# Backward of sliding-window attention on one core: its operations as one list per engine, ordered by positions

## The chip, the cores and the metric

The program runs on one core of a Trainium2 chip. The metric is the device time of one execution in microseconds, from the first to the last instruction and what lies around them. The core has five instruction queues that run side by side and wait for one another through semaphores: TensorE (PE, matmuls; PEld in the profile is its weight loads), VectorE (DVE), ScalarE (ACT), GpSimd (POOL) and SyncE (SP, which only issues DMAs here). Each queue runs its instructions in the order in which the program has them.

## The reference, cut to what matters

Four layers run forward and then backward: linear attention (A), sliding-window attention (B), A, B. The change touches only the backward of the scores of layer kind B, which runs twice.

```python
def _B_ref(x, wqkv, wo):
    B, S, D = x.shape                  # 1, 2048, 640
    H = 32; Dh = D // H; W = 256       # 32 heads of 20
    qkv = (lambda x, *d: x.transpose(*d))((x @ wqkv).reshape(B, S, 3, H, Dh), 2, 0, 3, 1, 4)
    q, k, v = qkv[0], qkv[1], qkv[2]
    scores = jnp.einsum("bhqd,bhkd->bhqk", q, k) * (Dh ** -0.5)
    idx = jnp.arange(S)
    mask = (idx[:, None] - idx[None, :] >= 0) & (idx[:, None] - idx[None, :] < W)
    scores = jnp.where(mask[None, None], scores, -1e9)
    p = _softmax(scores, axis=-1)
    o = jnp.einsum("bhqk,bhkd->bhqd", p, v)
    ...
x = x + _A_ref(_layernorm(x, axis=-1), A_wqkv, A_wo)
x = x + _B_ref(_layernorm(x, axis=-1), B_wqkv, B_wo)
x = x + _A_ref(_layernorm(x, axis=-1), A_wqkv, A_wo)
x = x + _B_ref(_layernorm(x, axis=-1), B_wqkv, B_wo)
...
_out, _vjp = jax.vjp(_f, A_x, A_wqkv, A_wo, B_wqkv, B_wo)
_grads = _vjp(grad_out)
```

For each head the backward needs the weights e = exp(scores) again, the product dP = dO V^T (its inputs are prepared beforehand so that dS = dP * e), and from them dQ = dS K, dK = dS^T Q and dV = e^T dO.

## The kernel before, in words

`B_attn_bwd` does this part. It is called twice, for layer 3 (761 us to 1088 us in the profiled execution) and for layer 1 (1501 us to 1822 us); what lies before, between and after the two calls is the same code in both kernels.

**Tiling.** The sequence is cut into 16 tiles of 128 rows (`TT`), the 32 heads into 8 groups of 4 (`G`). A head has 20 columns, padded to 32 (`HPAD`), so that the four heads of a group lie in four strips of 32 rows of the PE array. A query tile t meets the key tiles t-2, t-1 and t: three blocks of 128x128 to a head. A group has 15 steps (`NB`; the first step takes query tiles 0 and 1 together), a call has 120 steps (`NS`). A step n works on two pairs of heads, p = 0 and p = 1, numbered h = 2n + p. "Position" below is n modulo 15.

**The operations of a pair**, with the lines of the kernel before:

- S: scores, two matmuls from `QT` and `KT`, each in a strip of 32 rows (L1563). They go to `pair0`, `pair1` or `pair2` in PSUM, two banks each.
- X: exp on ACT, from that bank to `e_sb` (L1583). M: two masks on POOL (L1587, L1590).
- DP: two matmuls from `dOT` and `VT` (L1563) into the same PSUM bank, after X has read it.
- DS: `ds_sb` = bank * `e_sb` on DVE (L1598). It frees the bank for S of the pair three further on.
- T: dS turned. Either six transposes on PE into `dsT_ps`, a single PSUM bank (L1611), and then C, a copy to `dsT` on ACT (pair 0) or on DVE (pair 1) (L1615); or one DMA transpose from `ds_sb` to `dsT`, issued by SP (in the helper at L326). Pair 0 is always turned on PE. Pair 1 is turned by DMA at 11 of 15 positions (all but 0, 2, 4 and 6), and by PE in the last six steps of a call.

**The operations of a unit** (one group and one tile t, three steps after the step that has query tile t):

- A: the narrow products. For each head up to nine matmuls of 128x128 against 32 columns (L1627 for dQ, L1631 for dK and dV) into `dqvk_ps`, one PSUM bank. They need `dsT` of the step three back (for pair 1 in heads 2 and 3).
- EV: DVE scales the bank into `dqkv` (L1636) and frees it. 128 EV belong to a call.

Two units, the last of a group and the first of the next, fall into position 2.

**The order** is written out in one loop over h under `tc.manual_schedule`; the engines' queues take the operations in the order of the code. In one turn of the loop: DS(h), S(h+3), DP(h+2), X(h+3) with M(h+3), T(h), then the DVE copy of the pair before, EV of the unit that is done, the ACT copy if h is even, and half of the unit's heads. So PE has S and DP of two different pairs next to each other, then six transposes (if any), then 18 narrow matmuls; that twice a step. The `ds_sb` ring has 5 buffers, `e_sb` 7, `dsT` 8, `dsT_ps` and `dqvk_ps` one each.

**SP** also issues the seven slab loads of the next group, four of them DMA transposes (`QTg`, `KTg`, `VTg`, `dOTg`) and three plain (`Ksl`, `Qsl`, `dOsl`), at positions 0, 2, 4, ..., 12, each ahead of the step's own dS; and weights (`wq`) at positions 9 and 14 (layer 3) or in the last group (layer 1). In the last group the next phase's first loads stand between them in SP's queue.

## Time and profile before

| what | us |
|---|---|
| three timed runs | 2197.92, 2197.25, 2187.54 (median 2197.25) |
| the profiled execution | 2190.22 |
| its span, first to last instruction | 2188.3 |
| first to last EV, layer 3 | 776.2 to 1088.5 |
| first to last EV, layer 1 | 1514.8 to 1821.3 |
| DS on DVE, one | 0.949 |
| X on ACT, one | 0.812 |
| C on ACT, one; on DVE | 0.797; 0.558 |
| a mask on POOL, one | 0.406 |
| EV on DVE, one | 0.408 |
| DMA transpose of dS: issue on SP, median | 1.24 |

Every line of a timeline below has the start, the duration, engine, line, operation, output and input with their shapes, the number of instructions merged into it, and in brackets how long the engine stood idle before it and who ended that. The start of one EV to the start of the next is the length of a step.

### The profile page before, as it was taken

How to read it: one execution, taken by the hardware profiler on the slowest of the kernel's cores; microseconds unless marked ns; L12 is line 12 of the kernel's file. 1: busy time of each engine (PE TensorE's matmuls, PEld its weight loads, DVE VectorE, ACT ScalarE, POOL GpSimd, SP SyncE). 2: the span in 40 equal slices, each digit the busy share in tenths (PEclk: the TensorE clock that was granted, in tenths of full speed). 3: DMA queues.
4: the chain of work that ended last, by engine and by line, in shares of the span. 5: the costliest groups of instructions: out<-in, count | busy, mean ns of one | idle time of the engine just before them, and what ended most of it. 6: DMA issues, size and time to landing. Idle time of an engine off the chain costs nothing. (4 is left out here: it accounts for less than half of the span.)

```text
span 2188.3 us, 67939 instructions
## 1 busy us (share of the span) xinstructions
PE 1996.8 (91%) x27856; PEld 1392.4 (64%) x27856; DVE 1435.9 (66%) x2950; ACT 1200.1 (55%) x1981; POOL 879.3 (40%) x1850
## 2 busy tenths in 40 slices
PE   6878899879999789999899999998999999998999
PEld 4655666556666566676656667646676666666774
DVE  6766667577776288888734458705888885444651
ACT  4627777627778388888622223314989882120430
POOL 1015556516777355555423213202656551231220
PEclk9989999999999899999999999999999999999999
DMA  7459989569998499989888799936989996999954
GB/s 261 166 140 198 196 190 191 120 188 199 213 201 193 100 154 158 161 162 162 170 192 182 188 193 213 194 94 131 160 149 162 148 183 147 195 191 220 187 114 102
DMA packets 947802, 375.70 MB, mean 172 GB/s; under 512 B 828321, under 2 KB 928289, under 8 KB 947105
## 3 DMA queue, kind: packets, MB, share of 16 engines
q1 hardware_dynamic: 869712, 297.55, 71.3%
q10 hardware_dynamic: 77776, 73.79, 11.2%
q8 instruction: 218, 3.57, 0.7%
q14 instruction: 96, 0.78, 0.1%
HBM read 106.56 MB, written 112.07 MB: 100 GB/s over the span
## 5 line engine op out<-in xcount | busy, mean ns | idle before, releaser
L1598 DVE TENSOR_TENSOR ds_sb<-pair,e_sb 128x768 bf16<-128x768 f32 x480 | 436.6, 949 | 26.6 <-PE pair L1563 22.9
L1583 ACT ACTIVATE e_sb<-pair 128x768 bf16<-128x768 f32 x480 | 386.4, 812 | 85.2 <-PE pair L1563 81.6
L807 POOL TENSOR_SCALAR_AFFINE_SELECT e_sb<-e_sb 128x384 bf16<-128x384 bf16 (+1 forms) x512 | 198.4, 406 | 369.5 <-ACT e_sb L798 341.2
L798 ACT ACTIVATE e_sb<-s_ps 128x1152 bf16<-128x1152 f32 (+2 forms) x256 | 273.8, 1069 | 108.9 <-PE s_ps L794 79.1
L1590 POOL TENSOR_SCALAR_AFFINE_SELECT e_sb<-e_sb 128x256 bf16<-128x256 bf16 x448 | 182.1, 406 | 246.6 <-ACT e_sb L1583 239.5
L1054 PE MATMUL dw_ps<-dqkv,om 128*128 128x480 bf16 x1280 | 268.8, 366 | 0.0
L1054 PEld LDWEIGHTS <-om 128*128 128x128 bf16 x1760 | 170.1, 98 | 152.0 <-DMA om<-o 9.0
L1242 POOL TENSOR_TENSOR gw<-w,gcar 128x640 f32<-128x640 f32 x64 | 89.4, 1398 | 427.6 <-ACT w L1239 413.7
L1587 POOL TENSOR_SCALAR_AFFINE_SELECT e_sb<-e_sb 128x256 bf16<-128x256 bf16 x512 | 206.5, 407 | 95.5 <-ACT e_sb L1583 95.2
L1054 PEld LDWEIGHTS <-dqT 128*128 128x128 bf16 x1920 | 186.8, 98 | 73.9 <-DMA dqT<-dqkv 0.6
L1615 ACT COPY dsT<-dsT_ps 128x768 bf16<-128x768 bf16 x240 | 191.2, 797 | 24.0 <-PE dsT_ps L1611 7.2
L1611 PE MATMUL dsT_ps<-ident,ds_sb 128*128 128x128 bf16 x1896 | 165.2, 225 | 17.0 <-ACT dsT L1615 15.4
L439 PE MATMUL mm_ps<-Wqkv_B,hnTB 128*128 128x320 bf16 x960 | 171.0, 310 | 8.1 <-DVE gcar L511 5.5
L1627 PEld LDWEIGHTS <-dsT 128*128 128x128 bf16 x2880 | 154.4, 97 | 37.5 <-issue 31.2
L1627 PE MATMUL dqvk_ps<-Ksl,dsT 128*128 128x32 bf16 x2160 | 168.3, 178 | 7.9 <-DMA dsT<-ds_sb 4.9
L1631 PE MATMUL dqvk_ps<-Qsl,ds_sb 128*128 128x32 bf16 x2160 | 165.4, 177 | 0.0
L1631 PE MATMUL dqvk_ps<-dOsl,e_sb 128*128 128x32 bf16 x2160 | 165.3, 177 | 0.0
L1611 PEld LDWEIGHTS <-ds_sb 128*128 128x128 bf16 x1896 | 116.7, 100 | 72.1 <-issue 70.3
L1631 PEld LDWEIGHTS <-ds_sb 128*128 128x128 bf16 x2880 | 145.2, 96 | 0.0
L1631 PEld LDWEIGHTS <-e_sb 128*128 128x128 bf16 x2880 | 144.8, 96 | 0.0
L812 POOL TENSOR_SCALAR_AFFINE_SELECT e_sb<-e_sb 128x512 bf16<-128x512 bf16 x224 | 142.6, 637 | 0.0
L801 ACT ACTIVATE e_sb<-s_ps 128x384 bf16<-128x384 f32 (+2 forms) x256 | 119.9, 469 | 39.1 <-PE s_ps L794 10.5
(209 smaller groups left out, 3949.5 us busy)
## 6 DMA issues: line engine op xcount, KB each, us to landing
qkvp<-qk_slab SPq DMA_DIRECT2D x64, 256.0 KB, 3.5
hn<-hn SPq DMA_DIRECT2D x64, 160.0 KB, 3.2
om<-hn SPq DMA_DIRECT2D x20, 512.0 KB, 5.3
qkvp<-v_slab SPq DMA_DIRECT2D x32, 256.0 KB, 3.7
o<-o SPq DMA_DIRECT2D x48, 160.0 KB, 3.2
om<-o SPq DMA_DIRECT2D x15, 512.0 KB, 5.1
Ksl<-qkvp SPq DMA_DIRECT2D x12, 512.0 KB, 5.3
Qsl<-qkvp SPq DMA_DIRECT2D x12, 512.0 KB, 5.1
```

The costliest lines, as they stand in the source:

```text
L439: nc.tensor.matmul(ps.t[:, w0:w0 + width], lhsT=lhsT(), rhs=rhs(), start=start, stop=stop)
L798: op("ACT", av(3 * nkt * P), lambda: nc.scalar.activation(e.t[:, 0:3, 0:nkt, :], s3.t[:, :, 0:nkt * P].rearrange("p h (i q) -> p h i q", q=P),
L807: nc.gpsimd.affine_select(out=v, in_=v, compare_op=ALU.is_ge, fill=0.0, base=0, pattern=[[0, h1 - h0], [1, P]], channel_multiplier=-1)
L1054: nc.tensor.matmul(ps.t[:, w0:w0 + width], lhsT=lhsT(), rhs=rhs(), start=start, stop=stop)
L1583: nc.scalar.activation(e, PR[h][:, :, 0:3 * P].rearrange("p i (j q) -> p i j q", q=P), ACT.Exp, scale=self.c_att)
L1587: nc.gpsimd.affine_select(out=e[:, :, j, :], in_=e[:, :, j, :], compare_op=ALU.is_ge, fill=0.0, base=0, pattern=[[0, 2], [-1, P]], channel ...
L1590: nc.gpsimd.affine_select(out=e[:, :, j, :], in_=e[:, :, j, :], compare_op=ALU.is_ge, fill=0.0, base=-1, pattern=[[0, 2], [1, P]], channel ...
L1598: nc.vector.tensor_mul(DS[n][:, hs], PR.pop(h)[:, :, 0:3 * P].rearrange("p i (j q) -> p i j q", q=P), E[n][:, hs])
L1611: nc.tensor.transpose(ps[:, i, j, :], DS[n][:, 2 * p + i, j, :], self.ident)
L1615: (nc.vector.tensor_copy if h % 2 else nc.scalar.copy)(TSB[h], TPS.pop(h))
L1627: nc.tensor.matmul(a[:, 0, hh, :], lhsT=TSB[2 * n + hh // 2][:, hh % 2, j, :], rhs=ld[g]["K"][:, k, cs], start=(i == 0), stop=(i == len(dq ...
L1631: nc.tensor.matmul(a[:, 1 + x, hh, :], lhsT=src[n][:, hh, j, :], rhs=ld[g][rhs][:, q, cs], start=(i == 0), stop=(i == len(dkv) - 1))
```

## The change

The loop that wrote the order out is gone. Each operation is put into the list of its engine with a position in steps, n plus a constant from the table `ATTN`; each list is sorted by position. The lists are then emitted so that an operation comes after those that it depends on. The positions fix, for each step n in the middle of a group, these cyclic orders:

- PE: DP0(n+1), A heads 1 and 0 of unit n, S0(n+2), DP1(n+1), T1(n) if it is on PE, A heads 3 and 2 of unit n, S1(n+2), T0(n+1).
- DVE: DS0(n+1), C1(n) if any, EV(n), DS1(n+1).
- ACT: C0(n), X0(n+2), X1(n+2). POOL: M0(n+2), M1(n+2).
- SP: the DMA transpose of pair 1 at DS1's position; a slab load for the next group just after that of its own step.

At position 2, which has two units, each unit's four heads stand together: T0(2), the first unit, DP0(3), S0(4), DP1(3), the second unit, S1(4), T0(3).

The table `TURN` says by position how the two pairs are turned: A is PE with a copy on ACT, D is PE with a copy on DVE, F is the DMA. Pair 1 is F at all positions but 5, 6 and 10, and D in the last three steps of a call. That makes 93 DMA transposes of dS in a call where there were 82, and 147 groups of six PE transposes where there were 158; the DVE copies go from 38 to 27. All other operations, their shapes and their numbers are as before, and so are the rings of buffers.

```diff
+    ATTN = dict(S=[-1.794, -1.317],
+                X=[-1.605, -1.429],
+                DP=[-1.045, -0.72],
+                DS=[-0.982, -0.288],
+                T=[-0.152, 0.293],
+                CA=[0.37, 0.207],
+                CD=[-0.808, 0.062],
+                A=[0.152, -0.038, 0.437, 0.345],
+                A2=[-0.11, 0.608],
+                EV=0.26,
+                EV2=[-0.158, 0.258])
+    TURN = ["AF", "AF", "AF", "AF", "AF", "AD", "AD", "AF", "AF", "AF", "AD", "AF", "AF", "AF", "AF"]
...
-                if p == 1 and n % NB not in (0, 2, 4, 6) and n < NS - 6:
+                if by == "F":
                     self.dma_t(t.rearrange("p i j q -> p (i j) q"),
                                DS[n][:, 2 * p:2 * p + 2].rearrange("p i j q -> p (i j q)"))
                     return
...
+            for n in range(NS):
+                for p in range(2):
+                    h = 2 * n + p
+                    by[h] = TURN[n % NB][p] if n < NS - 3 else "AD"[p]
+                    op("PE", n + AT["S"][p], ("S", h), lambda h=h: score(h), [("DS", h - 3)] if h >= 3 else [])
+                    op("ACT", n + AT["X"][p], ("X", h), lambda h=h: weights(h), [("S", h)] + (users(n - 7) if not p else []))
+                    op("POOL", n + AT["X"][p], ("M", h), lambda h=h: masks(h), [("X", h)])
+                    op("PE", n + AT["DP"][p], ("DP", h), lambda h=h: by_head(h, PR[h], "dOT", "VT"), [("X", h)])
+                    op("DVE", n + AT["DS"][p], ("DS", h), lambda h=h: product(h),
+                       [("DP", h), ("M", h)] + (users(n - 5) if not p else []))
+                    free = [("DS", h)] + users((h - 8) // 2)
+                    if by[h] == "F":
+                        op("SP", n + AT["DS"][p], ("T", h), lambda h=h: turned(h, "F"), free)
+                    else:
+                        op("PE", n + AT["T"][p], ("T", h), lambda h=h: turned(h, "P"), free)
+                        op("ACT" if by[h] == "A" else "DVE", n + AT["CA" if by[h] == "A" else "CD"][p], ("C", h),
+                           lambda h=h: copied(h, by[h]), [("T", h)])
...
+                        at = AT["A2"][i] if len(us) == 2 else AT["A"][hh]
+                        op("PE", n + at, ("A", g, t, hh), lambda g=g, t=t, hh=hh: narrow(g, t, hh), deps)
+                    op("DVE", n + (AT["EV2"][i] if len(us) == 2 else AT["EV"]), ("EV", g, t),
+                       lambda g=g, t=t: evac(g, t), [("A", g, t, hh) for hh in range(4)])
...
+                    op("SP", (g - 1) * NB + 2 * i - 0.001, ("L", g, i), lambda g=g, i=i: slab(g, i), gone if g > 1 else [])
...
+            queue = {e: [name for _, _, name in sorted(v, key=lambda it: it[:2])] for e, v in lists.items()}
...
-                for h in range(2 * (NS + 4)):
-                    n, p = divmod(h, 2)
...
-                    if here:
-                        dve_ds(h)
-                        mm_s(h + 3)
-                        mm_dp(h + 2)
-                        act_exp(h + 3)
-                        turn(h)
...
-                    if (h - 1) % 2:
-                        copy_t(h - 1)
-                    for o in done:
-                        evac(*o)
...
-                    if not p:
-                        copy_t(h)
...
-                        mm_acc(*o, heads)
...
+                while any(queue.values()):
+                    before = len(done)
+                    for names in queue.values():
+                        while names and all(d in done for d in made[names[0]][1]):
+                            done.add(names[0])
+                            made[names.pop(0)][0]()
+                    assert len(done) > before
```

More of the change, by code (lines that the diff above doesn't have):

```diff
@@ L1565, in by_head, with op, score, weights @@
                                          start=True, stop=True, tile_position=(HPAD * hh, 0))
-            def mm_s(h):
-                if h < 2 * NS:
-                    PR[h] = pps.tile([P, 2, 512], F32, name=f"pair{h % 3}")
-                    by_head(h, PR[h], "QT", "KT")
-            def mm_dp(h):
-                if h < 2 * NS:
-                    by_head(h, PR[h], "dOT", "VT")
-            def act_exp(h):
-                if h >= 2 * NS:
-                    return
+            lists = {e: [] for e in ("PE", "DVE", "ACT", "POOL", "SP")}
+            made, bank = {}, {}
+            def op(eng, at, name, f, deps=()):
+                lists[eng].append((at, len(lists[eng]), name))
+                made[name] = (f, list(deps))
+            def score(h):
+                PR[h] = pps.tile([P, 2, 512], F32, name=f"pair{h % 3}")
+                by_head(h, PR[h], "QT", "KT")
+            def weights(h):
                 n, p = divmod(h, 2)
-                if n not in E:
+                if not p:
                     E[n] = pe.tile([P, 4, 3, P], BF, name="e_sb", bufs=7)
+                nc.scalar.activation(E[n][:, 2 * p:2 * p + 2],
+                                     PR[h][:, :, 0:3 * P].rearrange("p i (j q) -> p i j q", q=P), ACT.Exp,
+                                     scale=self.c_att)
+            def masks(h):
+                n, p = divmod(h, 2)
                 e = E[n][:, 2 * p:2 * p + 2]
-                nc.scalar.activation(e, PR[h][:, :, 0:3 * P].rearrange("p i (j q) -> p i j q", q=P), ACT.Exp,
-                                     scale=self.c_att)
                 for j, (t, k) in enumerate(blocks(n)):
@@ L1591, in act_exp, with product @@
                                                 base=-1, pattern=[[0, 2], [1, P]], channel_multiplier=-1)
-            def dve_ds(h):
+            def product(h):
                 n, p = divmod(h, 2)
-                if n not in DS:
+                if not p:
                     DS[n] = pe.tile([P, 4, 3, P], BF, name="ds_sb", bufs=5)
@@ L1599, in dve_ds, with turned @@
                                      E[n][:, hs])
-            def turn(h):
+            def turned(h, by):
                 n, p = divmod(h, 2)
                 t = TSB[h] = pe.tile([P, 2, 3, P], BF, name="dsT", bufs=8)
-                if p == 1 and n % NB not in (0, 2, 4, 6) and n < NS - 6:
+                if by == "F":
                     self.dma_t(t.rearrange("p i j q -> p (i j) q"),
@@ L1611, in turn, with copied, narrow @@
                         nc.tensor.transpose(ps[:, i, j, :], DS[n][:, 2 * p + i, j, :], self.ident)
-            def copy_t(h):
-                if h in TPS:
-                    (nc.vector.tensor_copy if h % 2 else nc.scalar.copy)(TSB[h], TPS.pop(h))
-            def mm_acc(g, t, hhs):
+            def copied(h, by):
+                (nc.scalar.copy if by == "A" else nc.vector.tensor_copy)(TSB[h], TPS.pop(h))
+            def narrow(g, t, hh):
                 if (g, t) not in ACC:
@@ L1621, in mm_acc, with sources @@
                 a = ACC[g, t]
-                dq = [(k, *place(g, t, k)) for k in range(max(t - 2, 0), t + 1)]
-                dkv = [(q, *place(g, q, t)) for q in range(t, min(t + 3, TT))]
-                for hh in hhs:
-                    cs = slice(HPAD * hh, HPAD * (hh + 1))
-                    for i, (k, n, j) in enumerate(dq):
-                        nc.tensor.matmul(a[:, 0, hh, :], lhsT=TSB[2 * n + hh // 2][:, hh % 2, j, :],
-                                         rhs=ld[g]["K"][:, k, cs], start=(i == 0), stop=(i == len(dq) - 1))
-                    for x, (src, rhs) in enumerate(((DS, "Q"), (E, "dO"))):
-                        for i, (q, n, j) in enumerate(dkv):
-                            nc.tensor.matmul(a[:, 1 + x, hh, :], lhsT=src[n][:, hh, j, :],
-                                             rhs=ld[g][rhs][:, q, cs], start=(i == 0), stop=(i == len(dkv) - 1))
+                dq, dkv = sources(g, t)
+                cs = slice(HPAD * hh, HPAD * (hh + 1))
+                for i, (k, n, j) in enumerate(dq):
+                    nc.tensor.matmul(a[:, 0, hh, :], lhsT=TSB[2 * n + hh // 2][:, hh % 2, j, :],
+                                     rhs=ld[g]["K"][:, k, cs], start=(i == 0), stop=(i == len(dq) - 1))
+                for x, (src, rhs) in enumerate(((DS, "Q"), (E, "dO"))):
+                    for i, (q, n, j) in enumerate(dkv):
+                        nc.tensor.matmul(a[:, 1 + x, hh, :], lhsT=src[n][:, hh, j, :],
+                                         rhs=ld[g][rhs][:, q, cs], start=(i == 0), stop=(i == len(dkv) - 1))
+            def sources(g, t):
+                return ([(k, *place(g, t, k)) for k in range(max(t - 2, 0), t + 1)],
+                        [(q, *place(g, q, t)) for q in range(t, min(t + 3, TT))])
             def evac(g, t):
@@ L1639, in evac, with users @@
                     ACC.pop((g, t))[:, :, :, 0:DH], self.ckv.rearrange("p s (h d) -> p s h d", d=DH))
+            def users(n):
+                return [("A", n // NB, n % NB + 1, hh) for hh in range(4)] if n >= 0 else []
+            AT, TURN = self.ATTN, self.TURN
+            by = {}
+            for n in range(NS):
[15 more added lines that the diff above has]
+                           lambda h=h: copied(h, by[h]), [("T", h)])
             outs = {}
@@ L1644, in B_attn_bwd @@
                     outs.setdefault(g * NB + t + 2, []).append((g, t))
+            for n, us in outs.items():
+                for i, (g, t) in enumerate(us):
+                    dq, dkv = sources(g, t)
+                    for hh in range(4):
+                        pair = hh // 2
+                        deps = [("DS", 2 * m + pair) for _, m, _ in dkv]
+                        deps += [("T" if by[2 * m + pair] == "F" else "C", 2 * m + pair) for _, m, _ in dq]
+                        at = AT["A2"][i] if len(us) == 2 else AT["A"][hh]
+                        op("PE", n + at, ("A", g, t, hh), lambda g=g, t=t, hh=hh: narrow(g, t, hh), deps)
+                    op("DVE", n + (AT["EV2"][i] if len(us) == 2 else AT["EV"]), ("EV", g, t),
+                       lambda g=g, t=t: evac(g, t), [("A", g, t, hh) for hh in range(4)])
             if first is None:
@@ L1649, in B_attn_bwd, with slab @@
                 ld[0] = first
+            todo = {}
+            def slab(g, i):
+                if g not in todo:
+                    todo[g] = loads(g)
+                todo[g][i]()
+            for g in range(1, G):
+                for i in range(7):
+                    gone = [("DP", 2 * (g - 1) * NB - 1)] if i < 4 else [("A", g - 2, TT - 1, hh) for hh in range(4)]
+                    op("SP", (g - 1) * NB + 2 * i - 0.001, ("L", g, i), lambda g=g, i=i: slab(g, i), gone if g > 1 else [])
+                made["S", 2 * g * NB][1].extend(("L", g, i) for i in range(4))
+                for hh in range(4):
+                    made["A", g, 0, hh][1].extend(("L", g, i) for i in range(4, 7))
@@ new lines, in B_attn_bwd @@
+            ws = next_weights()
+            for i, f in enumerate(ws):
+                n = (i // 2) * NB + (9, 14)[i % 2] if l == 3 else NS - NB + 2 * i + 1
+                op("SP", n + 0.6, ("W", i), f)
+            if l == 3:
+                op("SP", NS, ("W", "kept"), lambda: nc.sync.dma_start(out=kept, in_=self.wq), [("W", len(ws) - 1)])
+            queue = {e: [name for _, _, name in sorted(v, key=lambda it: it[:2])] for e, v in lists.items()}
+            last = {}
+            for name in queue["PE"]:
+                if name[0] == "T":
+                    made[name][1].extend(last.get("T", []))
+                    last["T"] = [("C", name[1])]
+                if name[0] == "A":
+                    u = name[1:3]
+                    if last.get("u") != u:
+                        last["A"], last["u"] = [("EV", *last["u"])] if "u" in last else [], u
+                    made[name][1].extend(last["A"])
@@ L1650, in B_attn_bwd @@
+            done = set()
             with tc.manual_schedule(engines={mybir.EngineType.PE, mybir.EngineType.DVE, mybir.EngineType.SP,
                                              mybir.EngineType.Activation, mybir.EngineType.Pool}):
-                for h in range(3):
-                    mm_s(h)
-                    act_exp(h)
-                for h in range(2):
-                    mm_dp(h)
-                todo, done, weights = [], [], next_weights()
-                for h in range(2 * (NS + 4)):
-                    n, p = divmod(h, 2)
-                    here = n < NS
-                    if here and not p:
-                        if n % NB == 0:
-                            todo = loads(n // NB + 1) if n // NB + 1 < G else []
-                        if n % NB % 2 == 0 and todo:
-                            todo.pop(0)()
-                    if here:
-                        dve_ds(h)
-                        mm_s(h + 3)
-                        mm_dp(h + 2)
-                        act_exp(h + 3)
-                        turn(h)
-                        if p and weights and (n % NB in (9, 14) if l == 3 else n >= NS - NB and n % 2):
-                            weights.pop(0)()
-                            if l == 3 and not weights:
-                                nc.sync.dma_start(out=kept, in_=self.wq)
-                    if (h - 1) % 2:
-                        copy_t(h - 1)
-                    for o in done:
-                        evac(*o)
-                    done = []
-                    if not p:
-                        copy_t(h)
-                    units = outs.get(n, [])
-                    if len(units) == 2:
-                        units, heads = [units[p]], range(4)
-                    else:
-                        heads = (0, 1) if p == 0 else (2, 3)
-                    for o in units:
-                        mm_acc(*o, heads)
-                        if heads[-1] == 3:
-                            done.append(o)
```

## The prediction

> **What bounds the kernel now.** The chain that ended last holds a tenth of the span, all in the last phase, so it says nothing of these two calls. I went by stages, first the busy times in two stretches of layer 1's call.

> ```profile
> span 2188.3 us, 67939 instructions
> core 0: us, PE busy (x) PEld busy (x) DVE busy (x) ACT busy (x) POOL busy (x), PEclk, DMA share, GB/s
> 1600.00:1650.00 50.00, 46.23 (x1031) 35.10 (x1030) 44.77 (x65) 44.96 (x60) 30.31 (x80) 1.00 0.86 155
> 1650.00:1700.00 50.00, 46.30 (x1030) 34.69 (x1026) 44.38 (x66) 45.24 (x60) 30.17 (x79) 1.00 0.99 159
> ```

> PE, DVE and ACT are each busy for nine tenths and none is full (PE's ends are modelled, so its 46 us flatter it). That is the look of a loop through several queues. Next the lengths of the steps, from DVE's timeline (starts of EV):

> ```profile
> 1630.23 0.40 DVE L1636 TENSOR_TENSOR dqkv<-dqvk_ps,ckv 128x240 bf16<-128x240 f32 x1
> 1632.42 0.41 DVE L1636 TENSOR_TENSOR dqkv<-dqvk_ps,ckv 128x240 bf16<-128x240 f32 x1
> 1635.55 0.40 DVE L1636 TENSOR_TENSOR dqkv<-dqvk_ps,ckv 128x240 bf16<-128x240 f32 x1
> ...
> 1655.19 0.41 DVE L1636 TENSOR_TENSOR dqkv<-dqvk_ps,ckv 128x240 bf16<-128x240 f32 x1 [0.30 <-PE dqvk_ps L1631]
> 1657.63 0.41 DVE L1636 TENSOR_TENSOR dqkv<-dqvk_ps,ckv 128x240 bf16<-128x240 f32 x1 [0.30 <-PE dqvk_ps L1631]
> ...
> 1668.65 0.40 DVE L1636 TENSOR_TENSOR dqkv<-dqvk_ps,ckv 128x240 bf16<-128x240 f32 x1
> ```

> Steps with pair 1 by DMA (F steps) in a row take 1657.63 - 1655.19 = 2.44 us; one with pair 1 on PE and DVE (a D step) takes 1635.55 - 1632.42 = 3.13 (3.03 to 3.08 elsewhere; the F step after it 2.15 to 2.24). From 1630.23 to 1668.65 a whole group takes 38.42. What closes the 2.44? The timeline of one such step:

> ```profile
> 1655.08 0.33 PE L1563 MATMUL pair<-KTg,QTg 32*128 32x384 bf16 x2
> 1655.54 0.34 PE L1563 MATMUL pair<-VTg,dOTg 32*128 32x384 bf16 x2
> 1655.81 0.51 PE L1611 MATMUL dsT_ps<-ident,ds_sb 128*128 128x128 bf16 x6
> 1656.16 0.23 PE L1627 MATMUL dqvk_ps<-Ksl,dsT 128*128 128x32 bf16 x3
> 1656.41 0.80 ACT L1615 COPY dsT<-dsT_ps 128x768 bf16<-128x768 bf16 x1
> 1657.11 1.60 ACT L1583 ACTIVATE e_sb<-pair 128x768 bf16<-128x768 f32 x2
> 1657.98 0.11 PEld L1563 LDWEIGHTS <-slabA 32*128 32x128 bf16 x3 [0.35 <-issue]
> ```

> DP (1655.54) to T .27, T to the copy C on ACT .60, C to exp X .70, X to the next DP .87: together 2.44. So the F step is a loop DP, T, C, X, DP, closed only by the order: T stands right behind DP on PE, X right behind C on ACT. In a D step two sets of transposes share one bank `dsT_ps`, so the second also waits for ACT's copy (.85 after C begins) before half of A may go.

> **The change: what it removes.** C0(n) now stands one window behind T0(n), and the DP that waits for the next X comes a window later. The old loop then has T to C .60, C to X .75, X to DP .87 and PE from DP0 on to T0 (1.9, below), 4.1 us over two steps. It no longer binds.

> **What it adds: one row-tiled group.** S and DP of two pairs used to share PE's 32-row strips. From the starts in the timeline: S and DP together (1654.26) to the next narrow matmul (1654.54) .28; DP alone (1655.54) to T (1655.81) .27. A lone pair costs as much as two. Before, a step had two such groups; now three: DP0, S0 with DP1, S1. PE's F step, each price up to the next operation's start:

> - DP0 .27; A, 18 narrow matmuls, 1654.54 to 1655.08, .54; S0 with DP1 .28; A .54; S1 .27; T0 up to DP0 x.

> For x full clock shows only T up to narrow matmuls, .35 (1655.81 to 1656.16), below. Above: at half clock six transposes ran from 768.87 to the row-tiled 769.60, .73; S and DP together up to A take .44 at that clock (873.51 to 873.95) against .28, so .73 x .28/.44 = .46. I take .44: the next starts .07 before the last transpose ends, as at the other changes to and from the strips. [...]

> So an F step is 2.34 on PE, against 1.98 of work (2 x .28, 2 x .54, .35) in the old 2.44. At x = .35 it would be 2.25, at .46 2.36: over 14 steps and 16 groups -20 and +4 us.

> **Is anything slower than 2.34?** DVE: from DS0's start S1 follows after 1.00 (DS .949 and .05), then T0 .27, DP0 .44, A .27, .54, .28, EV .63 after A's second half starts, DS1 .32, DS0 .86: 4.61 over two steps, 2.31. Through the masks: S0 to X .38, X to M .88, two masks .77, DS0 .03, S1 1.00, T0 .27, DP0 .44, A .27, S0 .54: 4.58, 2.29. ACT: X, X, C at .71, .71 and .75 is 2.17. DVE's own work is 2.05. These lie right under PE's 2.34, so I keep 2.30 to 2.44 for an F step.

> D steps add T1, .35, and a wait: C0 starts behind X1 of the window before, ends some .12 after PE could start T1. 2.34 + .47 = 2.81. Here C1 on DVE stands ahead of EV and DS1; its .56 fits, since EV waits for A until 2.2 in that window. Position 2: A of 20 narrow matmuls .59, DP0 and S0 and DP1 in one mode .44, .13 for the first unit's EV (`dqvk_ps` is one bank), A of 28 .79, S1 .27, T0 .44: 2.66.

> A group: 11 x 2.34 + 3 x 2.81 + 2.66 = 36.8 against 38.42: 1.6, times 16 groups is 26. In the last six steps, all D before at 2.80 (1073.39 to 1076.19), two become F: 2 x .46 x 2 calls = 2. The 22 DVE copies (.56) and 132 transposes that go are inside these sums.

> **SP and the transfers.** 22 more DMA transposes, 1.24 of issue each, 27 us on SP, which has room: 12 x 1.24 + 4 x 2.2 + 3 x .58 = 25 of 37 us a group.

> ```profile
> L326 SPq DMA_TRANSPOSE dsT<-ds_sb x81: 1209/1243/3934, 1516.1 to 1801.2; - x81
> L326 SPq DMA_TRANSPOSE slabA<-qkvp x9: 1979/2132/4199, 1545.5 to 1709.7; - x9
> ...
> DMA to landing us min/median/max: 2.5/4.3/7.8
> ```

> The cover is the slack. Pair 1's narrow products come 3.6 windows after DS1 starts: 8.1 us, less .95, leaves 7.2 between dS and its use (6 at position 0, used three windows later by the group's first unit). At positions 0 to 4 five F steps in a row meet three slab loads: SP needs 5 x 1.24 + 3 x 2.2 = 12.8 in 12 us. T1 and T3 stand behind QT and KT, some 1 to 2 us late in issue, and land 2.5 to 5 after: 3.5 to 7. Nothing left over, but hidden; positions 5 and 6 are D and let SP catch up. If late, PE stops at A heads 3 and 2; behind them on PE wait S1 and T0, and EV on DVE. Before, in layer 1's whole call, this happened once:

> ```profile
> DVE dqkv L1636 <- PE dqvk_ps L1631: 18.9, 59, 1.0
> PE dqvk_ps L1627 <- DMA dsT<-ds_sb: 1.0, 1, 1.0
> ```

> At the end of layer 3's call it cost more: EV from 1062.43 to 1067.20, 4.77 where 2.39 is usual, with the next phase's loads in SP's queue ahead of dS. D at 5 and 6 may spare that, the new order may bring it elsewhere: -2.4 to +2.4, I take 0.

> **Sum.** 26 + 2 = 28 off the profiled 2190.2 (span 2188.3 and 1.9 around it): 2162. The median of the runs is 7 above that execution; I expect the runs between 2162 and 2169 and write 2166.

> **Rivals.**

> 1. *The loops close higher.* If the DVE and mask loops carry .1 to .15 more than I read (waits between queues in an order that no trace shows), F is 2.43 and D 2.95: 11 x 2.43 + 8.85 + 2.75 = 38.3, no change: 2190 to 2197. For it: three loops within .05 of PE. Against: each link is read from a row.
> 2. *dS by DMA comes late.* T1, T3 and one behind `Ksl` (whose neighbours took up to 6.2 to land, 1024.73 in layer 3) miss by 1 us each, in every group: 3.0 - 1.6 = +1.4, times 16, +22 on 2190: 2212. It turns to slower from 1.6 us lateness in a group. For it: the 7.2 and the 12.8 in 12 above. Against: after QT (1661.15) and KT (1665.75) the next dS landed within 2.9 and 2.5 of its issue.
> 3. *More than I think.* x is .35, which shortens PE and both loops alike: 20 more, 2142; with half of it 2152.
> 4. *It doesn't change the order as said.* Rows and counts are fixed by the lists; I leave it at 1 in 100, within "same".

> **How the numbers follow.** Forecast .57, rival 3 .14, rival 1 .14, rival 2 .15. The forecast's own range, F from 2.30 to 2.40 (14 x 16 steps, -9 and +13 on 2162 to 2169), is 2153 to 2182. The range that should hold 8 in 10 takes in most of rival 3, rival 1 and a third of rival 2: 2145 to 2204. 0.5% (11 us) is about what a measurement of this kernel can tell from no change. Of rival 1 .03 counts as faster and .11 as same, of rival 2 .02 as same and .13 as slower; so faster .74, same .13, slower .13.

> **What would show it.** Right: EV to EV 2.3 to 2.4 in rows of F steps, 2.8 in D steps, 36.8 a group; PE without waits there but DVE idle some .3 a step; the wait of T for ACT's copy nearly gone outside D steps. Wrong: narrow matmuls waiting for "DMA dsT<-ds_sb" at positions 3 to 7 and 11 to 13 (rival 2); EV steps of 2.43 with PE waiting for `ds_sb` (rival 1); T0 to DP0 not .44. What makes it wrong most easily is the transfers, whose price I know only from a less crowded order.

## The result and the profile after

Over 20 runs the changed kernel takes a median of 2203.13 us (2183.86 to 2245.21), the kernel before 2187.22 (2178.4 to 2197.92, 20 runs). The ratio is 1.0058, with 95% from 1.0037 to 1.0079: a little slower, where 2166 and faster was forecast. The ratios here leave out runs over 1.5% above the quickest of the same kernel (four of these 20; the median of the other 16 is 2200.3). The runs of the changed kernel spread over 61 us, those of the kernel before over 20.

The profiled execution of the changed kernel is the quickest of its 20 runs, 2183.86. Two lines of its page, the span with its instructions and the granted clock in 40 slices:

```profile
span 2182.1 us, 67718 instructions
PEclk9989999999999879999899999998999988999999
```

The clock of the kernel before:

```profile
PEclk9989999999999899999999999999999999999999
```

The two calls lie in slices 14 to 20 and 28 to 34. The kernel before had one 8 there, this one several 8s and a 7. From first to last EV (the scaling of a finished unit on DVE) the calls take 311.7 and 303.9 us (312.3 and 306.4 before).

First the part of the prediction that is a list of durations. An F step of layer 1's call at full clock, from PE's timeline (the loads of weights and most of the narrow matmuls left out):

```profile
1638.36 0.51 PE L1628 MATMUL dsT_ps<-ident,ds_sb 128*128 128x128 bf16 x6
1638.80 0.34 PE L1576 MATMUL pair<-VTg,dOTg 32*128 32x384 bf16 x2
1639.07 0.24 PE L1640 MATMUL dqvk_ps<-Ksl,dsT 128*128 128x32 bf16 x3
...
1639.62 0.33 PE L1576 MATMUL pair<-KTg,QTg 32*128 32x384 bf16 x2
1639.62 0.33 PE L1576 MATMUL pair<-VTg,dOTg 32*128 32x384 bf16 x2
1639.89 0.24 PE L1640 MATMUL dqvk_ps<-Ksl,dsT 128*128 128x32 bf16 x3
...
1640.44 0.34 PE L1576 MATMUL pair<-KTg,QTg 32*128 32x384 bf16 x2
1640.71 0.51 PE L1628 MATMUL dsT_ps<-ident,ds_sb 128*128 128x128 bf16 x6
```

T0 to DP0 .44, DP0 .27, A .55, S0 with DP1 .27, A .55, S1 .27: 2.35, with no idle time in brackets. Each link is within .01 of what the prediction gave it. The steps that follow from it, in DVE's timeline (starts of EV):

```profile
1680.18 0.40 DVE L1654 TENSOR_TENSOR dqkv<-dqvk_ps,ckv 128x240 bf16<-128x240 f32 x1
...
1684.84 0.41 DVE L1654 TENSOR_TENSOR dqkv<-dqvk_ps,ckv 128x240 bf16<-128x240 f32 x1 [0.21 <-PE dqvk_ps L1644]
1687.19 0.41 DVE L1654 TENSOR_TENSOR dqkv<-dqvk_ps,ckv 128x240 bf16<-128x240 f32 x1 [0.21 <-PE dqvk_ps L1644]
...
1701.54 0.41 DVE L1654 TENSOR_TENSOR dqkv<-dqvk_ps,ckv 128x240 bf16<-128x240 f32 x1 [0.21 <-PE dqvk_ps L1644]
1704.37 0.40 DVE L1654 TENSOR_TENSOR dqkv<-dqvk_ps,ckv 128x240 bf16<-128x240 f32 x1
1707.16 0.40 DVE L1654 TENSOR_TENSOR dqkv<-dqvk_ps,ckv 128x240 bf16<-128x240 f32 x1
...
1716.99 0.40 DVE L1654 TENSOR_TENSOR dqkv<-dqvk_ps,ckv 128x240 bf16<-128x240 f32 x1
```

F steps 2.35 (1687.19 - 1684.84), D steps 2.83 and 2.79, a group 36.81 (1680.18 to 1716.99; 38.38 before), DVE idle .2 a step. So at full clock the change does what was forecast. Now PE in the same kernel during the last group of layer 3:

```profile
1061.59 0.82 PE L1628 MATMUL dsT_ps<-ident,ds_sb 128*128 128x128 bf16 x6
1062.34 0.50 PE L1576 MATMUL pair<-VTg,dOTg 32*128 32x384 bf16 x2
1062.77 0.26 PE L1640 MATMUL dqvk_ps<-Ksl,dsT 128*128 128x32 bf16 x3
...
1063.37 0.50 PE L1576 MATMUL pair<-KTg,QTg 32*128 32x384 bf16 x2
1063.37 0.50 PE L1576 MATMUL pair<-VTg,dOTg 32*128 32x384 bf16 x2
1063.81 0.26 PE L1640 MATMUL dqvk_ps<-Ksl,dsT 128*128 128x32 bf16 x3
...
1064.40 0.50 PE L1576 MATMUL pair<-KTg,QTg 32*128 32x384 bf16 x2
```

The same operations, again without a gap, at half clock: T0 to DP0 .75, a strip group .43 or .44, A .60, together 3.25. The narrow matmuls hardly slow down (A .60 for .55), the strips (.43 or .44 for .27) and the transposes (T0 to DP0 .75 for .44) do. The busy times of that stretch, of an undisturbed one and of one in the last group of layer 1 (columns: window, its length, PE, PEld, DVE, ACT, POOL busy, granted clock, DMA share, GB/s):

```profile
1060.00:1076.00 16.00, 16.00 (x245) 10.23 (x242) 11.17 (x17) 10.90 (x15) 7.48 (x20) 0.50 0.78 190
1600.00:1650.00 50.00, 49.48 (x1067) 35.92 (x1065) 46.21 (x67) 46.82 (x63) 31.42 (x83) 1.00 1.05 170
1787.00:1807.00 20.00, 19.83 (x295) 13.12 (x296) 14.01 (x21) 12.29 (x16) 8.06 (x22) 0.50 0.69 126
```

PE is full and the clock is .50 all the while. In the two calls PE spends 108.8 us at half clock in stretches of up to 27.3 us; before it was 44.8 us in stretches of up to 10.2. (The clock records of this trace hold only 1.00 and .50, in 44 stretches; each but the last, which the trace ends, is a multiple of 3.413 us long, a window below.)

The transfers, rival 2 of the prediction: what PE waited for in layer 3's call (us in all, times, longest):

```profile
PE dqvk_ps L1640 <- DMA dsT<-ds_sb: 4.1, 5, 1.1
PE pair L1576 <- DVE ds_sb L1615: 2.9, 4, 0.9
```

The first of these in the kernel before, same call:

```profile
PE dqvk_ps L1627 <- DMA dsT<-ds_sb: 3.9, 4, 2.3
```

Five waits of 4.1 us together, and one of 1.8 in layer 1. Counting EV tells the unit that waited: the first two, which end at 852.17 and 892.28, are for pair 1 of position 0, with the least slack; the others are for positions 1, 3 and 4, and in layer 1 for 4. They come to 6.0 us, but the kernel before had 4.9 in its two calls (3.9 above, 1.0 in the prediction). By themselves the waits explain some 1 us, not the 22 that this rival was given.

### The profile page after: what moved, and what is told of

The parts are those of the page before. It is cut to its first block, busy times and chain, and to the rows that moved or that the text cites. A ratio compares the mean times of both kernels' runs of the same rounds, so it can differ in the third digit from the quotient of the medians.

```text
span 2182.1 us, 67718 instructions
## 1 busy us (share of the span) xinstructions
PE 2029.4 (93%) x27724; PEld 1389.1 (64%) x27724; DVE 1433.2 (66%) x2928; ACT 1203.3 (55%) x1981; POOL 879.2 (40%) x1850
## 5 line engine op out<-in xcount | busy, mean ns | idle before, releaser
L1615 DVE TENSOR_TENSOR ds_sb<-pair,e_sb 128x768 bf16<-128x768 f32 x480 | 440.3, 950 | 44.9 <-PE pair L1576 22.9
L1640 PEld LDWEIGHTS <-dsT 128*128 128x128 bf16 x2880 | 146.3, 97 | 87.0 <-issue 79.1
L1631 ACT COPY dsT<-dsT_ps 128x768 bf16<-128x768 bf16 x240 | 190.5, 794 | 4.8 <-PE dsT_ps L1628 4.8
L1628 PEld LDWEIGHTS <-ds_sb 128*128 128x128 bf16 x1764 | 111.6, 103 | 59.5 <-issue 57.4
L1644 PEld LDWEIGHTS <-ds_sb 128*128 128x128 bf16 x2880 | 145.7, 97 | 0.6
L1054 PE MATMUL mm_ps<-wq,dqT 128*128 128x320 bf16 x960 | 139.9, 303 | 0.0
```

The source lines that it names most:

```text
L1054: nc.tensor.matmul(ps.t[:, w0:w0 + width], lhsT=lhsT(), rhs=rhs(), start=start, stop=stop)
L1615: nc.vector.tensor_mul(DS[n][:, hs], PR.pop(h)[:, :, 0:3 * P].rearrange("p i (j q) -> p i j q", q=P), E[n][:, hs])
L1628: nc.tensor.transpose(ps[:, i, j, :], DS[n][:, 2 * p + i, j, :], self.ident)
L1631: (nc.scalar.copy if by == "A" else nc.vector.tensor_copy)(TSB[h], TPS.pop(h))
L1640: nc.tensor.matmul(a[:, 0, hh, :], lhsT=TSB[2 * n + hh // 2][:, hh % 2, j, :], rhs=ld[g]["K"][:, k, cs], start=(i == 0), stop=(i == len(dq ...
L1644: nc.tensor.matmul(a[:, 1 + x, hh, :], lhsT=src[n][:, hh, j, :], rhs=ld[g][rhs][:, q, cs], start=(i == 0), stop=(i == len(dkv) - 1))
```

## The experiments

Theory H (half clock): the third strip group and the waits leave PE too little to do at half clock to be granted the full one; a short stall drops the clock, and the new order can't bring it back. Theory D (DMA): the late dS costs the time directly. Theory O (order): the new order itself closes somewhere higher. Times are medians of all runs, with the ratio to the kernel before run beside them (its median 2184.0 to 2184.7 in each batch). The 3072 full columns a window in the expectations are H's bar for the next window's clock (full from there on, half under it): in the traces before and after, behind the first 100 us and with each matmul put into the window of its middle, it is wrong in 2 of 82 windows at half clock and 5 of 1136 at full (all 12 traces stand in the last section). A group is timed from its first EV to that of the next group unless said otherwise.

**1. The changed kernel again, for a second trace.** No edit.

> The changed kernel once more, for a second trace. Theory (clock): at full clock the group takes 36.8 us as in the first trace, and what varies between executions is the time at half clock: 2 x (1 - mean clock) x span. Where a window of 3.41 us at half clock holds less than 3072 columns of the PE array (columns x rows / 128), the next stays at half clock; F steps at half clock hold 2688 in 3.25 us, so 2823 a window, and can't get out. Expected: every stretch at half clock inside the two calls ends with the first window above about 3072, time = about 2135 us + 0.28 x time at half clock. Rival (late transfers): the time follows the waits of the narrow matmuls for dsT by DMA, and the clock is no more than their shadow; a slow execution then shows many us of such waits, a fast one few.

Measured: 2220.39 us (2206.52 to 2227.49, 4 runs), ratio 1.0153 (1.0094 to 1.0211). The profiled execution took 2219.12 with 244.2 us of half clock inside the calls. Its clock by slices:

```profile
PEclk9989999999999876679999999997699997999999
```

The first matmuls after two of the waits, from PE's timeline (waiting time and who ended it in brackets):

```profile
815.75 0.21 PE L1640 MATMUL dqvk_ps<-Ksl,dsT 128*128 128x32 bf16 x1 [1.88 <-DMA dsT<-ds_sb]
...
904.14 0.21 PE L1640 MATMUL dqvk_ps<-Ksl,dsT 128*128 128x32 bf16 x1 [0.89 <-DMA dsT<-ds_sb]
```

The busy times of a stretch behind the first wait and of one in layer 1:

```profile
816.00:850.00 34.00, 34.00 (x511) 21.40 (x508) 23.62 (x33) 23.17 (x29) 14.57 (x38) 0.50 0.78 140
1600.00:1650.00 50.00, 49.53 (x1068) 35.90 (x1066) 46.07 (x67) 46.90 (x62) 31.30 (x82) 1.00 1.02 161
```

The clock falls at 815.4, inside a wait of 1.88 us for pair 1's `dsT`, and stays down for 51.2 us with PE busy all the time; it falls again at 904.1, at the end of a wait of .89, and stays down for 61.4. In these stretches every F step takes 3.25 and every D step 3.89, and a group, from last EV to last EV, 51.2 to 52.2 instead of 36.8. Undisturbed groups are as fast as in the first trace (36.82 to 36.87). So one kernel has 36.8 and 52 in one execution, which O can't give, and .89 us of waiting is followed by some 17 us lost (61.4 x .28, worked out below), which D can't give.

**2. The split alone, in the kernel before.** The transposes are put between S and DP, so that S and DP of a turned pair no longer share the strips: three strip groups in an F step and four in a D step, and nothing else of the change.

```diff
                         mm_s(h + 3)
+                        turn(h)
                         mm_dp(h + 2)
                         act_exp(h + 3)
-                        turn(h)
```

> The kernel before, with T(h) moved between S(h+3) and DP(h+2), so that S and DP are row-tiled groups of their own wherever pair h is turned on PE; places and number of the DMA transposes are those of before. Theory (clock): at half clock an F step then takes about 3.25 us on PE instead of 3.07, 2688 columns in it are 2823 a window and below 3072, so stretches at half clock last longer than the 3.4 to 10.2 us of before (some of 17 us or more), the mean clock falls under 0.965 and the timed runs spread over more than 20 us. Rival (late transfers, places of the DMA steps): nothing of this changes, mean clock 0.97 as before.

Measured: 2424.25 us (2416.74 to 2429.01, 4 runs), ratio 1.1091 (1.1048 to 1.1134). Its clock by slices:

```profile
PEclk9989899999997555555699999985555555999999
```

The busy times of its two calls:

```profile
770.00:1190.00 420.00, 419.10 (x6068) 254.50 (x6066) 281.06 (x391) 282.36 (x351) 179.47 (x469) 0.50 0.62 119
1620.00:2050.00 430.00, 427.75 (x6211) 260.74 (x6210) 287.23 (x402) 284.97 (x355) 181.06 (x472) 0.50 0.58 111
```

PE is busy for 419.10 of 420.00 us, and the clock is half from the first group to the last of both calls. F steps take 3.25, as in the changed kernel's bad stretches, D steps 4.43. An order that starts at half clock and never gets out of it, without a wait beyond the first steps: this is what H describes, in pure form. It went further than H expected (stretches of some 17 us, runs spread over more than 20): the whole call is lost, and the runs lie within 12 us.

**3. The same, with useless work.** Once a group, at position 7, 20 matmuls of the identity with itself (128 columns each) into the bank `dqvk_ps`, which the next unit overwrites; nothing is left out of the computation.

```diff
+                    if not p and n < NS and n % NB == 7:
+                        a = pps.tile([P, 3, 4, HPAD], F32, name="dqvk_ps")
+                        for i in range(20):
+                            nc.tensor.matmul(a[:, i % 3].rearrange("p h d -> p (h d)"), lhsT=self.ident,
+                                             rhs=self.ident, start=True, stop=True)
```

> The kernel before with S and DP split as in split_before, and 20 useless matmuls (128 columns, never read) at position 7 of every group. Theory (clock): the split order stayed at half clock through both calls only because it can't get out, not because its order is slow at full clock. The useless matmuls fill a window beyond 3072, so the clock returns in the first group of each call, and later stretches end at the next position 7; mean clock 0.95 or more instead of 0.806 and 2190 to 2260 us instead of 2424, with 16 x 1.1 us of work added. If the split order were slow by itself (waits between the queues): 2424 plus 16 x 1.1 to 2.1, about 2450.

Measured: 2227.25 us (2219.1 to 2235.77, 4 runs), ratio 1.0187 (1.0137 to 1.0238): 320 more matmuls make the kernel of experiment 2 197 us faster. Its clock by slices:

```profile
PEclk9989999999999789699999999997999999999999
```

Two starts of EV in its layer 1, from DVE's timeline:

```profile
1645.54 0.41 DVE L1636 TENSOR_TENSOR dqkv<-dqvk_ps,ckv 128x240 bf16<-128x240 f32 x1 [0.21 <-PE dqvk_ps L1631]
1647.88 0.41 DVE L1636 TENSOR_TENSOR dqkv<-dqvk_ps,ckv 128x240 bf16<-128x240 f32 x1 [0.21 <-PE dqvk_ps L1631]
```

A group now takes 39.96 instead of 53.43, although the step with the burst, an F step of 2.34, grows to 3.68. F steps are 2.34 (2.44 in the kernel before): the split as such is no loss at full clock. That leaves only the clock between experiments 2 and 3 (mean .806 and .965).

**4. The third strip group taken back out of the changed kernel.** T0 goes ahead of S1, so that S1 and the next DP0 stand together and a step has two strip groups again.

```diff
-                T=[-0.152, 0.293],
+                T=[-0.33, 0.293],
```

> The changed kernel with T0 moved ahead of S1, so that S1 and DP0 of the next window share a row-tiled group again (two groups a step as before); everything else, the twelve DMA steps among it, as changed. Theory (clock): at half clock an F step takes about 2.8 us and holds 2688, 3280 a window, so half clock ends after one or two windows; mean clock 0.97 or more and runs within 15 us. At full clock each merged group has to wait for an exp (S to X 0.38, X to DP 0.87, twice a step: 2.48), so F steps are 2.45 to 2.5 and a group about 38.5: 2180 to 2195 us in all. Rival (late transfers): the stalls on dsT stay, with them the low clock of 0.94 to 0.96, and with slower F steps the time is 2200 or more.

Measured: 2216.14 us (2213.08 to 2220.85, 4 runs), ratio 1.0144 (1.0109 to 1.0178). Half right. Half clock in the calls fell from 108.8 us (244.2 in the second trace) to 59.9, longest stretch 19.0, as H wants, though the stretches that stay (17.1 at the start of each call, 19.0 at the end of layer 1's) are longer than the one or two windows expected. But the time rose: the group at full clock is 40.33, not 38.5, since D steps became 3.17 to 3.50 (most F steps 2.40 to 2.52, about as expected). The place of T0 matters to D steps in a way I hadn't worked out, so this run shows that half clock in the calls fell, and not what that is worth.

**5. The layer-3 weights elsewhere in SP's queue.** At positions 5 and 10 instead of 9 and 14, to take them from ahead of position 0's dS.

```diff
-                n = (i // 2) * NB + (9, 14)[i % 2] if l == 3 else NS - NB + 2 * i + 1
+                n = (i // 2) * NB + (5, 10)[i % 2] if l == 3 else NS - NB + 2 * i + 1
```

> The changed kernel with the weight transposes of layer 3 at positions 5 and 10 (where pair 1 is on PE) instead of 9 and 14. Both theories: the dS of position 0 no longer stands behind a weight load, so the waits of 0.7 to 1.3 us at the first unit of a group in layer 3 (852, 892, 937, 980 us in the first trace) go. Clock theory: with these triggers gone the stretches at half clock in the middle of layer 3's call go too, though the waits themselves are only 3 us in all; mean clock up by 0.005 to 0.015, the median 5 to 15 us under that of the changed kernel. Late transfers as such: 3 us less.

Measured: 2191.97 us (2180.43 to 2211.67, 10 runs), ratio 1.0037 (1.0002 to 1.0072). A miss for the stalls: in layer 3 they were fewer (three, 2.8 us) but not gone (one still at position 0, two now at 11 and 13), and in the profiled execution a single one, .98 us near 1005, is followed by 92.2 us of half clock. The median is 8 to 11 us under the changed kernel's (2200.3 and 2203.1), within the 5 to 15 that H expected and above D's 3; but the two come from different batches, and the intervals of their ratios overlap, so this decides little. Fewer stalls don't help reliably while one is enough.

**6. Useless work in the changed kernel.** 20 matmuls that nobody reads at position 7 of each group, as in experiment 3.

```diff
+            for n in range(7, NS, NB):
+                op("PE", n - 0.0385, ("F", n), lambda: fill(20), [("EV", n // NB, n % NB - 3)])
```

> The changed kernel with 20 useless matmuls (identity by identity, 128 columns, into the free bank of the narrow products, never read) at position 7 of every group. At full clock they cost 20 x 0.055 = 1.1 us a group, 18 us in all. Theory (clock): at half clock they fill a window beyond 3072 columns, so no stretch at half clock in the middle of a call runs on past position 7, none is longer than about 45 us, and the step after them is at 2.35 again; mean clock 0.955 to 0.97, the slow executions go, median 2185 to 2200 although 18 us of work were added. Rival (late transfers make the loss): 18 us slower than the changed kernel, 2220 to 2240.

Measured: 2200.66 us (2194.21 to 2207.3, 5 runs), ratio 1.0075 (1.005 to 1.0101), just above the range that H expected (2185 to 2200) and well below D's (2220 to 2240). The burst costs 1.33 a group (3.64 against 2.31), 21 us for 16 groups, and the half clock in the calls is 68.2 us; the runs spread over 13 us instead of 61 (five runs against 20). It buys back about what it costs and no more; the narrower spread is what H wants, from few runs.

**7. Useless work only where PE is idle anyway**, at the start of each call: 60 (layer 3) or 26 (layer 1) matmuls ahead of the first DP, 14 ahead of each of the next four S.

```diff
+            for i, (at, k) in enumerate(((-1.046, 60 if l == 3 else 26), (-0.3171, 14), (0.2059, 14), (0.6829, 14), (1.2059, 14))):
+                op("PE", at, ("F", i), lambda k=k: fill(k))
```

> The changed kernel with useless matmuls (identity by identity, 128 columns, never read) only where PE stands idle at the start of each call: 60 (layer 3) or 26 (layer 1) ahead of the first DP, 14 ahead of the next four S. At full clock 14 last 0.77 us, which is the wait there. Theory (clock): the first windows of a call keep 3072 columns or come back at once, the first group takes 37 to 38 us in both calls instead of 38 to 49; 5 to 15 us off the median of the changed kernel, stretches later in the calls are not changed. Rival (late transfers): no gain, or up to 3 us lost.

Measured: 2189.71 us (2176.54 to 2198.9, 10 runs), ratio 1.0008 (.9983 to 1.0033). The first groups, from their first to their last EV, take 35.50 and 35.76 where they took 39.9 and 38.7 in the first trace and 38.1 and 48.8 in the second. The stalls by DMA are still there (5.0 and 2.0 us), each but one of .28 followed by 7 to 31 us of half clock: 85.1 in the calls. The median is 11 to 13 us under the changed kernel's, where H expected 5 to 15.

**8. Start filled, weights at positions 5 and 6, and pair 1 on PE in the last 12 steps.**

```diff
-                    by[h] = TURN[n % NB][p] if n < NS - 3 else "AD"[p]
+                    by[h] = TURN[n % NB][p] if n < NS - 12 else "AD"[p]
...
-                n = (i // 2) * NB + (9, 14)[i % 2] if l == 3 else NS - NB + 2 * i + 1
+                n = (i // 2) * NB + (5, 6)[i % 2] if l == 3 else NS - NB + 2 * i + 1
```

> The changed kernel with three things against the low clock: the useless matmuls at the start of a call, the weight transposes of layer 3 at positions 5 and 6 (pair 1 on PE there) and pair 1 on PE in the last 12 steps of a call (3 before), where the next phase's loads make dS late. Theory (clock): full clock through nearly both calls, groups of 36.8, last group 40; mean clock 0.968 or more, 2165 to 2178 us, faster than both. Rival (late transfers): 6 steps more on PE cost 3 us a call, the waits that go bring 3 to 6 us; within 5 us of the changed kernel.

Measured: 2177.27 us (2161.56 to 2189.29, 10 runs), ratio .9957 (.9924 to .999). Two stretches of half clock stay in layer 3, 37.5 us from 837.4 and 30.7 from 1001.2, with three late transfers (2.0 us). These are of positions 7 and 9 (twice); position 0 has none here.

**9. The same, with pair 1 of position 0 on PE and DVE as well**, so that the transfer with the least slack is gone. This makes a D step of an F step in each group.

```diff
-    TURN = ["AF", "AF", "AF", "AF", "AF", "AD", "AD", "AF", "AF", "AF", "AD", "AF", "AF", "AF", "AF"]
+    TURN = ["AD", "AF", "AF", "AF", "AF", "AD", "AD", "AF", "AF", "AF", "AD", "AF", "AF", "AF", "AF"]
```

> As best1, with pair 1 on PE at position 0 as well (the dS that the first unit of a group needs a step sooner than others). Costs 0.47 us a group at full clock, 7.5 us in all. Theory (clock): the last trigger in the middle of layer 3's call goes; the runs lie within 12 us, mean clock 0.97, 2170 to 2182 us; better than best1 only if that one still falls to half clock at a group's first unit.

Measured: 2162.14 us (2160.19 to 2167.71, 4 runs), ratio .9895 (.987 to .9919): the fastest kernel here, below what was expected. Its clock by slices:

```profile
PEclk9989999999999899999999999999999999999999
```

The busy times of a stretch of each call:

```profile
810.00:850.00 40.00, 39.48 (x844) 28.70 (x840) 37.05 (x54) 37.14 (x49) 24.95 (x66) 1.00 1.12 174
1600.00:1650.00 50.00, 49.15 (x1044) 35.94 (x1043) 46.46 (x68) 46.04 (x62) 30.60 (x80) 1.00 1.02 161
```

No wait for `dsT` by DMA is left in either call, half clock inside the calls is 5.6 us, every group from the second to the seventh takes 37.27 or 37.28. This order has .48 more work a group than the changed kernel (37.28 against 36.80) and is 38 to 41 us faster, with a spread of 8 us in four runs. What position 0 itself brings is not shown: the late transfers of experiment 8 were elsewhere, and four of that kernel's ten runs (2161.56 to 2166.79) were as quick as these.

**10. Experiment 9 without the useless work at the start.**

```diff
-            for i, (at, k) in enumerate(((-1.046, 60 if l == 3 else 26), (-0.3171, 14), (0.2059, 14), (0.6829, 14), (1.2059, 14))):
-                op("PE", at, ("F", i), lambda k=k: fill(k))
```

> best2 without the useless matmuls at the start of a call. Theory (clock): each call starts at half clock (PE waits for the first loads and exps) and gets out only by chance in the first group or two, since F steps hold 2823 a window there; first groups of 38 to 50 us instead of 36.0; nothing to trigger it later. Mean clock 0.96 to 0.978, 2168 to 2190 us, 6 to 25 us above best2's 2162 and with a wider spread (best2: 2160 to 2168). If the start fill did nothing: 2162.

Measured: 2181.8 us (2171.24 to 2254.16, 10 runs), ratio .9972 (.9946 to .9999). Half clock is back: 20.5 us at the start of each call and 34.1 us from 1023.6 (one late transfer of 1.0 us, of position 7), 79.1 in the calls. The kernel without the filled start is 18 us slower (2180.4 for the eight runs behind the ratio, less 2162.1; 20 with all ten). In the trace the two starts hold 41.0 us of half clock, some 11 us lost (x .28), about as much as experiment 7 gained; the rest follows the late transfer, which the filling doesn't touch.

## Why the prediction was wrong

**Right: the steps.** F 2.34 was 2.34 to 2.35, x .44 was .44, D 2.81 was 2.79 to 2.83, the group 36.8 was 36.80 to 36.87 wherever the clock was full. Position 2 was 2.70 (two EV steps of 1.35) for 2.66. The loops through DVE, ACT and POOL stayed below PE; rival 1 is out. Rival 3 needed x = .35 and is out too.

**Half right: the transfers.** `dsT` came late where the prediction saw the least slack: position 0, given 6 us, and positions 1 and 3, behind QT and KT; besides, at position 4 in the last group of each call. The waits came to 6.0 us against 4.9 before, 1.1 more, where 0 was taken and 2.4 was the bound: as a direct cost that holds. Rival 2 had the place but a price of 3 us a group for waits in every group. What nobody priced is what follows a wait.

**Wrong: the sum.** The step that failed is "26 + 2 = 28 off the profiled 2190.2". It sets a sum at full clock against an execution that holds 120.5 us of half clock (44.8 of it in these calls), and so takes that time to be unchanged. It was not. The time at half clock of a run follows from its mean clock c as 2(1 - c) times its span. Over the 20 runs of the changed kernel it goes from about 175 to 417 us, median 258; for 46 runs of the kernel before, beside the experiments, its median is 109. A line through the 20 points rises by .268 us for each us at half clock (correlation .98), which is what the steps say: (3.25 - 2.35)/3.25 = .28. At 109 us, below all 20 points, the line drawn on stands at 2166. So by this estimate the forecast is the time that the kernel would have if it kept the clock of the kernel before, and the extra 149 us at half clock cost 40.

**The account of the profiled execution.** The forecast of 28 us off the calls' 312.3 + 306.4 gave 590.7; they took 615.6. Of these 24.9, 62 us more at half clock between first and last EV (86.5 against 24.9) at .28 are 17, and 1.1 more of waiting for `dsT` brings it to 18; some 7 us stay unexplained. The 2 us expected of the last six steps are among what was lost: both last groups ran partly at half clock (17.1 us from 1059.8, 20.5 us from 1786.8), behind waits for `dsT` of 1.1 and 1.8 us.

**Why the clock stays down.** Counted from the program and the row of an F step: 36 narrow matmuls of 32 columns, six transposes of 128 and eight strip matmuls of 384 columns on a quarter of the rows, 1152 + 768 + 768 = 2688 full columns; a D step has 768 more, 3456. In 3.413 us at half clock the changed order gets 2688 x 3.413/3.25 = 2823 through in F steps and 3456 x 3.413/3.89 = 3032 in D steps; the old order, 2688 x 3.413/3.07 = 2988 in F steps (three of them at half clock took 3.12, 3.07 and 3.07) and more in the D steps between. Over all 12 traces, windows below 3000 are nearly always followed by half clock (717 of 732) and those above 3160 by full clock (6514 of 6515); a bar at 3072 between them is wrong in 29 of 784 windows at half clock and 20 of 6562 at full (table in the last section). So at half clock the new order lies below the bar in F steps, about at it in D steps, and leaves half clock only at some of its D steps or at position 2: the 51.2 us stretch of the second trace ends at position 2, the 61.4 and 68.3 us ones behind the D step at position 5. In experiment 2 both kinds of step lie below, 2823 in F steps and 3456 x 3.413/4.43 = 2663 in D steps, and it never gets out. The old order sits close under the bar and gets over it at its next D step, within 10.2 us. It stalls too, but cheaply: its longest wait for `dsT`, 2.27 us up to 1066.50 in layer 3's last group, is followed by a single window at half clock, and one of .99 up to 1038.18 by none. At full clock both are far above (2688 x 3.413/2.35 = 3904, and /2.44 = 3760 for the old order); all 6353 windows above 3160 at full clock were followed by another at full. So nothing happens until a stall, and then .89 us was enough, with 61.4 us at half clock behind it. The third strip group was costed by its time at full clock, .27, and by that it was right; what it costs is the way back.

No rival named the clock, although the profile before showed 10.2 us at half clock in the middle of layer 3's call, and its half-clock rows were used for x. The question that was missing is how the order that comes does at half clock, and what brings it out.

What stays open: why D steps became 3.17 to 3.50 in experiment 4; what the 7 us are; and how much of the wide spread in 20 runs comes from the place of the windows and how much from transfers that land earlier or later, which no run here separates.

## What to carry to other kernels

Before costing a change to a PE order at full clock, cost one step at half clock too, and count the full columns that it gets through in a window: here an order with 2823 a window in its F steps at half clock paid for a wait of .89 us with 61.4 us at half clock. If a kernel's runs spread widely on one core, compare the granted clock of the runs before looking for a longer loop (over the 20 runs here the time at half clock and the run's time have a correlation of .98). Idle PE time at the start of a stage may be worth filling with matmuls that nobody reads (some 11 us in experiment 10), and half a microsecond more work in a group can be cheaper than a transfer that is late once (.48 in each of 16 groups is 7.7 us, against some 17 lost behind the wait of .89).

## What the runs showed of the hardware

The next window's clock against the full columns (columns x rows/128) that PE streamed in a window of 3.413 us, counted from the matmul rows and the clock records of the 12 traces here, all windows behind the first 100 us:

| full columns | at half clock: next half / next full | at full clock: next half / next full |
|---|---|---|
| below 3000 | 548 / 5 | 169 / 10 |
| 3000 to 3160 | 43 / 26 | 11 / 19 |
| above 3160 | 1 / 161 | 0 / 6353 |

In the second trace a wait of .89 us was followed by the drop; in the kernel before one of .99 was not. In experiment 2 the clock stayed at half for 420 us with PE busy for 419. In these traces the amount streamed in a window tells what comes next; how long PE waited doesn't.

The size is a surprise: in experiment 3, 320 useless matmuls took a kernel from 2424.25 to 2227.25 us, by keeping the clock.
